# Pooling attention, then a token-mixing MLP on one core: the first batch loads and pools v in another way

## The chip, the cores and the metric

The kernel runs on one core of a Trainium2 chip. The metric is the device time of one execution in microseconds (us). The kernel before takes 377.52 us, the median of three runs (377.23 to 377.54). The core has five engines that work side by side, each through its own queue in order: TensorE (PE in the profile, PEld for its weight loads), VectorE (DVE), ScalarE (ACT), GpSimd (POOL) and SyncE (SP), which issues most transfers. ScalarE and GpSimd can issue transfers as well.

## The reference

The inputs are q, k and v of shape 8 x 8 x 576 x 64 (batch, heads, tokens, head size) and the weights of a small MLP block. Tokens of k and v are averaged in groups of eight, so each of the 576 queries attends to 72 pooled keys. Then tokens are mixed by a 576 x 576 matrix, and an MLP of 512 to 2048 to 512 follows.

```python
def _attn_ref(q, k, v):
    B, H, S, D = q.shape          # 8, 8, 576, 64
    pool = 8
    Sp = S // pool                # 72
    k_p = k.reshape(B, H, Sp, pool, D).mean(axis=3)
    v_p = v.reshape(B, H, Sp, pool, D).mean(axis=3)
    scores = 1.0 / np.sqrt(D) * np.matmul(q, k_p.transpose(0, 1, 3, 2))
    scores = scores - np.max(scores, axis=-1, keepdims=True)
    attn = np.exp(scores)
    attn = attn / (np.sum(attn, axis=-1, keepdims=True) + 1e-09)
    return np.matmul(attn, v_p).astype(np.float32)

def _moe_ref(x, alpha1, beta1, w_tok, alpha2, beta2, w_ch1, w_ch2, lam):
    a1 = alpha1 * x + beta1
    tok = np.einsum('ts,bsd->btd', w_tok, a1)
    u = x + lam * tok
    a2 = alpha2 * u + beta2
    ch = np.maximum(a2 @ w_ch1, 0.0) @ w_ch2
    return (u + lam * ch).astype(np.float32)
```

## The kernel before

Every batch passes through the same steps. Names in the profile are those of the tiles in this code. The attention steps of one batch (`u` is a half of the heads, `hp` a pair of heads, `h` a head):

```python
def load_qk(b, u, behind=None):            # q and k of four heads, tokens 0 to 511
    raw = work.tile([P, 2, 4, 4, D], FP, tag="qk_raw", bufs=2, name="qk_raw")
    if behind is not None:
        behind.memset(raw[:, :, 0, 0, 0:1], 0.0)     # keeps the load behind this point of a queue
    for i, src in enumerate((q, k)):
        nc.sync.dma_start(...)
# load_rem: tokens 512 to 575 of q and k, all heads, four small transfers on SyncE

def load_v(b, u, parts=(0, 1)):            # v in f32, one group of 8 tokens on a partition: 72 partitions
    if parts[0] == 0:
        st1[b]["v"][u] = work.tile([SPG, 4, 8, D], FP, tag="v_u", bufs=2, name="v_u")
    ...
        nc.sync.dma_start(...)

def cast_q(b, u, copy): ...                # q to bf16
def sum_k(b, u, eng):                      # four neighbouring tokens of k become one
    eng.tensor_tensor(out=raw[:, :, 0:2], in0=raw[:, :, 0:2], in1=raw[:, :, 2:4], op=ALU.add)
    eng.tensor_tensor(out=bf, in0=raw[:, :, 0], in1=raw[:, :, 1], op=ALU.add)

def att_F(b, hp): ...                      # q transposed on TensorE, copied to qT by ScalarE
def att_Frem(b, us, copy): ...             # the same for tokens 512 to 575
def att_K(b, u, copy): ...                 # k pooled and transposed by TensorE, copied to kpT

def att_V(b, hp):                          # eight tokens of v become one, by three sums on VectorE
    t = st1[b]["v"][hp // 2][:, 2 * (hp % 2):2 * (hp % 2) + 2]
    for n in (4, 2):
        nc.vector.tensor_tensor(out=t[:, :, 0:n], in0=t[:, :, 0:n], in1=t[:, :, n:2 * n], op=ALU.add)
    nc.vector.tensor_tensor(out=vp1_pool[hp][:, :, 0:64], in0=t[:, :, 0], in1=t[:, :, 1], op=ALU.add)

def att_S(b, h):                           # scores, exp on ScalarE
    ET = ET_pool[2 * r + hh]               # four score buffers
    ...
def att_AV(b, h):                          # scores times pooled v, divided by their sum on VectorE
    ...
    nc.vector.reciprocal(out=rec, in_=av[:, :, 64:65])
    nc.vector.tensor_tensor(out=x[:, :, dd:dd + D], in0=av[:, :, 0:64], in1=rec..., op=ALU.mult)
def att_X(b, h0, h1, eng=nc.vector): ...   # xs = x * lam * alpha1, in bf16, for the token mixing
```

`mix_T` mixes the tokens of one chunk on TensorE (it needs all of xs), adds x on VectorE (`u_sb`) and scales by alpha2 (`u_bf`); `mix_uT` transposes the chunk; `mlp_A` is the first product of the MLP, `mlp_B` the second, in four parts, of which part g needs `w2[g]`. `scale_w2(g)` multiplies `w2[g]` by lam on VectorE:

```python
def scale_w2(g):
    nc.vector.tensor_tensor(out=w2[g], in0=w2[g],
                            in1=lam_bc.unsqueeze(1).to_broadcast((P, 4, DM)), op=ALU.mult)
```

The first batch has a program of its own, the head of the kernel. Its transfers are issued as q, k, v (main), remainders, v (rest), q, k, v on SyncE, with alpha1, lam, beta1, alpha2 and beta2 on GpSimd's queue:

```python
broadcast(1, lamal_bc)                     # a vector to all partitions, by TensorE
cast_q(0, 0, nc.vector.tensor_copy)
att_F(0, 0); att_F(0, 1)
broadcast(0, lam_bc)
sum_k(0, 0, nc.gpsimd)
for i, p0 in ((0, 64), (1, 0)):            # the row beta1 * lam of xs
    nc.vector.tensor_tensor(out=xs_pool[i][p0:p0 + 1, 4, :], ...)
cast_rem(0, nc.gpsimd, nc.vector.tensor_copy)
att_Frem(0, (0,), nc.vector.tensor_copy)
att_K(0, 0, nc.scalar.copy)
for h in range(4):
    att_S(0, h)
nc.vector.tensor_tensor(out=lamal_bc, in0=lamal_bc, in1=lam_bc, op=ALU.mult)
load_wtok()
att_V(0, 0); att_V(0, 1)
broadcast(2, al2_bc); setup_vectors()
for h in range(4):
    att_AV(0, h)
sum_k(0, 1, nc.gpsimd)
for g in range(4): load_w1(g)              # cast to bf16 by GpSimd's transfers
for g in range(4): load_w2(g)
cast_q(0, 1, nc.scalar.copy)
att_F(0, 2); att_Frem(0, (1,), nc.scalar.copy); att_F(0, 3); att_K(0, 1, nc.scalar.copy)
att_X(0, 0, 2); att_X(0, 2, 4)
att_V(0, 2); att_V(0, 3)
# ... scores and products of heads 4 to 7, w_tok transposed, att_X(0, 4, 6, nc.gpsimd), att_X(0, 6, 8)
mix_T(0, 0, nc.gpsimd); ...; mix_T(0, 1, nc.gpsimd); mix_T(0, 2); mix_T(0, 3)
# ...
load_qk(1, 0, nc.vector); load_rem(1); load_v(1, 0); load_qk(1, 1); load_v(1, 1)
# ... mlp_A(0, 0) to mlp_A(0, 3)
```

From then on the steps of the next batch are woven into the MLP of the one before, by slots: a list of (slot, step) is sorted and run in that order. The slots of batch 1, and of w2, in the first MLP block (`n == 0`, `b == 1`):

```python
todo = [(11.9, cast_rem)]
for u in range(2):
    at = 10.0 + 4.8 * u                    # cast_q at `at`, sum_k at `at + 0.1`, on GpSimd
    for r in range(2):
        at = 12.7 + 4.6 * u + 1.6 * r      # att_F at `at`, att_V at `at + 0.5`,
                                           # for r == 1 att_Frem at + 0.1, att_K at + 0.4 (VectorE copies)
for h in range(8):
    at = 17.0 + 0.9 * h                    # att_S at `at`, att_AV 1.6 later, att_X after each odd head
                                           # (on GpSimd for h < 5, else on VectorE)
for c in range(5):
    at = 26.2 + 0.9 * c                    # mix_T
# mlp_A(0, j) at slot j from 4 on, mlp_B(0, m) part p at 16 + 4 * p + m, mix_T(0, 4) at 11.4
for g in range(4):
    todo.append((4.2 + 1.7 * g, lambda g=g: scale_w2(g)))
```

Of the kernel before, what the change touches and what calls it, by code (L numbers as in the profile page):

```python
# [14 lines left out]
P = 128  # L15
SPG = 72
# [7 lines left out]
def kernel(  # L24
# [100 lines left out]

    wt_bf = const.tile([P, 5 * S + 64], BF, tag="wt_bf", name="wt_bf")
    nc.vector.memset(wt_bf[:, 4 * S:], 0.0)
# [11 lines left out]
    vecs = const.tile([65, 4, DM], FP, tag="vecs", name="vecs")  # L139
# [4 lines left out]
    nc.gpsimd.memset(start, 0.0)  # L144
    nc.scalar.activation(out=start[:, 1:2], in_=start[:, 0:1], func=AF.Exp, bias=0.0, scale=1.0)
    new_batch(0)
    load_qk(0, 0)
    load_v(0, 0, (0,))
    load_rem(0)
    load_v(0, 0, (1,))  # L150
    load_qk(0, 1)
    load_v(0, 1)


    for i, src in ((1, moe_alpha1), (0, moe_lam)):
        n = 65 if i in (0, 3) else 1
        nc.gpsimd.dma_start(out=vecs[0:n:64, i],
                            in_=src.unsqueeze(0).to_broadcast((1 + n // 65, DM)))
# [6 lines left out]
    nc.vector.memset(pool_main, 0.125)  # L165
    pool_each = const.tile([P, 32, 4], BF, tag="pool_each", name="pool_each")
# [4 lines left out]
    for t, n, width in ((pool_main, 64, 2),):  # L171
        nc.gpsimd.affine_select(out=t, in_=t, compare_op=ALU.is_ge, fill=0.0, base=0,
                                pattern=[[-width, n]], channel_multiplier=1)
        nc.gpsimd.affine_select(out=t, in_=t, compare_op=ALU.is_ge, fill=0.0, base=width - 1,
                                pattern=[[width, n]], channel_multiplier=-1)
    each4 = pool_each.rearrange("p (g a) j -> p g a j", a=4)
# [4 lines left out]
                            fill=1.0, base=0, pattern=[[-1, P]], channel_multiplier=1)  # L181
    nc.vector.memset(ones_bf, 1.0)
# [3 lines left out]

    nc.gpsimd.dma_start(out=vecs[0:65:64, 3], in_=moe_beta1.unsqueeze(0).to_broadcast((2, DM)))
    nc.gpsimd.dma_start(out=vecs[0:1, 2], in_=moe_alpha2.unsqueeze(0))
    nc.gpsimd.dma_start(out=b2row, in_=moe_beta2.rearrange("(c p) -> c p", p=P))

    vp1_pool, kpT_pool, ET_pool = [], [], []
    for i in range(4):
        t = const.tile([SPG, 2, 66], F16, tag=f"vp1_{i}", name=f"vp1_{i}")
        nc.vector.memset(t, 8.0)
        vp1_pool.append(t)
        if i < 2:
            t = const.tile([P, 2, 2, SPG], BF, tag=f"kpT_{i}", name=f"kpT_{i}")
            nc.vector.memset(t, 0.0)
            kpT_pool.append(t)
        t = const.tile([SPG, S + 128], F16, tag=f"ET_{i}", name=f"ET_{i}")  # L200
        nc.vector.memset(t[:, 0:64], 1.0)
        nc.vector.memset(t[:, 64 + S:], 1.0)
        ET_pool.append(t)
# [10 lines left out]
    nc.vector.tensor_reduce(out=pool_rem, in_=pool_each, op=ALU.max, axis=AX.X)  # L214
# [80 lines left out]
    def att_F(b, hp):  # L295


        st = st1[b]
        u, r = hp // 2, hp % 2
        ps_q = gp("ps_q").bitcast(BF)  # L300
        for c in range(4):
            nc.tensor.transpose(  # L302
                out=ps_q[:, 128 * c:128 * c + 128],
                in_=st["q"][u][:, c, 2 * r:2 * r + 2].rearrange("p h d -> p (h d)"),
                identity=identity_bf)
        if r == 0:
            st["qT"][u] = work.tile([P, 2 * S], BF, tag="qT", bufs=4, name="qT")
        nc.scalar.copy(out=st["qT"][u][:, 640 * r:640 * r + 512], in_=ps_q[:, 0:512])
# [39 lines left out]

    def att_S(b, h):
        st = st1[b]  # L350
        u, r, hh = h // 4, h // 2 % 2, h % 2
        ET = ET_pool[2 * r + hh]
# [131 lines left out]
    new_batch(1)  # L484
    broadcast(1, lamal_bc)
    cast_q(0, 0, nc.vector.tensor_copy)
    att_F(0, 0)
    att_F(0, 1)
    broadcast(0, lam_bc)
    sum_k(0, 0, nc.gpsimd)  # L490
    for i, p0 in ((0, 64), (1, 0)):
        nc.vector.tensor_tensor(out=xs_pool[i][p0:p0 + 1, 4, :], in0=vecs[p0:p0 + 1, 3],
                                in1=vecs[p0:p0 + 1, 0], op=ALU.mult)
    cast_rem(0, nc.gpsimd, nc.vector.tensor_copy)
    att_Frem(0, (0,), nc.vector.tensor_copy)
    att_K(0, 0, nc.scalar.copy)
    for h in range(4):
        att_S(0, h)
    nc.vector.tensor_tensor(out=lamal_bc, in0=lamal_bc, in1=lam_bc, op=ALU.mult)
    load_wtok()  # L500
    att_V(0, 0)
    att_V(0, 1)
    broadcast(2, al2_bc)
    setup_vectors()
    for h in range(4):
        att_AV(0, h)
    sum_k(0, 1, nc.gpsimd)
    for g in range(4):
        load_w1(g)
    for g in range(4):  # L510
        load_w2(g)
    cast_q(0, 1, nc.scalar.copy)
    att_F(0, 2)
    att_Frem(0, (1,), nc.scalar.copy)
    att_F(0, 3)
    att_K(0, 1, nc.scalar.copy)
    att_X(0, 0, 2)
    att_X(0, 2, 4)
    att_V(0, 2)
    att_V(0, 3)  # L520
    for h in (4, 5, 6):
        att_S(0, h)
    att_AV(0, 4)
    att_S(0, 7)
    att_AV(0, 5)
    setup_wtok(0, nc.scalar.copy)
    att_X(0, 4, 6, nc.gpsimd)
    setup_wtok(1, nc.scalar.copy)
    att_AV(0, 6)
    att_AV(0, 7)  # L530
    setup_rowsum(0)
    setup_wtok(2, nc.scalar.copy)
    setup_rowsum(1)
    setup_wtok(3, nc.scalar.copy)
    att_X(0, 6, 8)
# [4 lines left out]
    mix_T(0, 2)  # L540
    mix_T(0, 3)
# [5 lines left out]
    load_rem(1)  # L547
    load_v(1, 0)
    load_qk(1, 1)
# [44 lines left out]
    for n in range(NBLK):  # L594
# [7 lines left out]
        if n == 0:  # L602
# [5 lines left out]
            for g in range(4):  # L608
                todo.append((4.2 + 1.7 * g, lambda g=g: scale_w2(g)))
# [43 lines left out]
```

The softmax here doesn't subtract the row's maximum and nothing guards it: scores larger than these inputs give would overflow.

## Time and profile before

| engine | busy us | share of the span | instructions |
|---|---|---|---|
| TensorE | 357.1 | 95% | 2283 |
| TensorE weight loads | 194.3 | 51% | 2283 |
| VectorE | 228.4 | 61% | 462 |
| ScalarE | 187.8 | 50% | 382 |
| GpSimd | 78.0 | 21% | 94 |

The profile's span is 377.4 us. The inputs read from memory are 38.04 MB, and the profile gives 126 GB/s over the span for reads and writes together. A share of busy time is an average over stages that have different limits; the chain that ended last, the waits and the busy time by stretches say what limits each stage. In a timeline line the columns are the start, the duration, the engine, the line of the kernel, the operation with its output and input tiles and shapes, how many instructions are merged, and in brackets the idle time before them with what ended it. In the chain they are start, duration, engine, tile and line.

### The profile page before, as it was taken

Reading aid. Unit: us, or ns where it says so; the run is one execution under the profiler, and the core shown is the slowest. Engines: PE = TensorE matmul, PEld = TensorE weight load, DVE = VectorE, ACT = ScalarE, POOL = GpSimd, SP = SyncE. Lnnn points to the kernel's source line nnn. Section 1 sums busy time; section 2 is a strip of 40 time slices with the busy share of each in tenths; the row PEclk is TensorE's granted clock in tenths of the full one; section 3 lists DMA queues with packets and bytes.
Section 4 is the critical chain, followed back from the end, with each engine's and each line's share of the span. In section 5 each row is a group of like instructions: output and inputs, shape, how many; then the busy total and the mean of one; then the engine's idle time right before and its main releaser. Section 6 shows DMA issues by size and latency. Waiting matters only on the chain.

```text
span 377.4 us, 5931 instructions
## 1 busy us (share of the span) xinstructions
PE 357.1 (95%) x2283; PEld 194.3 (51%) x2283; DVE 228.4 (61%) x462; ACT 187.8 (50%) x382; POOL 78.0 (21%) x94
## 2 busy tenths in 40 slices
PE   2879999799999999999999999999999999999995
PEld 0465655355655555555545554455455544544542
DVE  4797748785687569748964697469755784011011
ACT  1574766128822792269415941586148613712710
POOL 7563243900700070008000700071000000000000
PEclk9999999899999999999999999999999999999999
DMA  8999999418430753156315632383100001002012
GB/s 199 226 191 213 263 208 259 92 56 265 113 105 36 213 138 83 57 174 168 90 58 154 188 91 57 103 237 92 56 30 0 29 29 57 0 30 83 0 48 65
DMA packets 34845, 43.02 MB, mean 114 GB/s; under 512 B 2360, under 2 KB 24956, under 8 KB 34816
## 3 DMA queue, kind: packets, MB, share of 16 engines
q1 hardware_dynamic: 31744, 37.76, 36.7%
q0 software_dynamic: 3072, 4.87, 7.3%
q8 instruction: 18, 0.29, 0.4%
q14 instruction: 11, 0.09, 0.1%
HBM read 38.04 MB, written 9.44 MB: 126 GB/s over the span
## 4 chain that ended last, share of the span: by engine, by line
PE 87%; DVE 8%; DMA 2%; issue 1%; POOL 1%; ACT 0%; POOLq 0%; DVEq 0%
PE ps_h L452 33%; PE ps_ch L470 31%; PE ps_tok L421 12%; PE ps_sc L356 4%; PE ps_uT L436 2%; DMA vecs<-in_moe_beta_dram 2%; PE ps_av L372 2%; PE ps_q L302 2%; DVE x_tm L380 2%; DVE v_u L344 2%; DVE xs L387 1%; DVE vp L346 1%; DVE u_sb L423 1%; DVE u_bf L425 1%; PE ps_bias L290 1%
## 5 line engine op out<-in xcount | busy, mean ns | idle before, releaser
L470 PE MATMUL ps_ch<-w,Hj 128*128 128x512 bf16 x576 | 140.7, 380 | 0.0
L452 PE MATMUL ps_h<-u_fm,w 128*128 128x512 bf16 (+2 forms) x592 | 133.6, 373 | 0.0
L457 ACT ACTIVATE Hj<-ps_h,bias_cols 128x512 bf16<-128x512 f32 x144 | 98.8, 689 | 43.5 <-PE ps_h L452 42.6
L452 PEld LDWEIGHTS <-w 128*128 128x128 bf16 x592 | 64.0, 114 | 48.6 <-issue 0.3
L470 PEld LDWEIGHTS <-Hj 128*128 128x128 bf16 x576 | 54.5, 98 | 50.8 <-issue 1.6
L438 ACT COPY u_fm<-ps_uT 128x512 bf16<-128x512 bf16 x36 | 21.1, 586 | 94.3 <-PE ps_uT L436 94.1
L475 DVE TENSOR_TENSOR u_sb<-u_sb,ps_ch 128x512 f32<-128x512 f32 x36 | 24.5, 684 | 55.7 <-PE ps_ch L470 55.5
L358 ACT ACTIVATE ET<-ps_sc 72x288 f16<-72x288 f32 x128 | 44.9, 408 | 19.6 <-PE ps_sc L356 19.5
L421 PE MATMUL ps_tok<-xs,wtT 128*128 128x512 bf16 (+1 forms) x200 | 50.5, 385 | 2.6 <-DVE xs L387 2.6
L423 DVE TENSOR_TENSOR u_sb<-x_tm,ps_tok 128x512 f32<-128x512 f32 (+1 forms) x40 | 27.5, 687 | 30.7 <-PE ps_tok L421 30.5
L344 DVE TENSOR_TENSOR v_u<-v_u 72x512 f32<-72x512 f32 x64 | 43.2, 674 | 2.6 <-DMA v_u<-in_v_dram 1.1
L380 DVE TENSOR_TENSOR x_tm<-ps_av,rec 128x320 f32<-128x320 f32 x64 | 31.5, 492 | 2.3
L107 POOL CAST rem_q<-rem_raw 128x256 bf16<-128x256 f32 x7 | 3.7, 528 | 140.6 <-PE ps_h L452 92.5
L421 PEld LDWEIGHTS <-wtT 128*128 128x128 bf16 (+1 forms) x200 | 19.4, 99 | 25.9 <-DVE xs L387 2.5
L338 DVE CAST kpT<-ps_kp 64x144 bf16<-64x144 f32 x28 | 8.5, 305 | 38.4 <-PE ps_kp L334 38.2
L356 PE MATMUL ps_sc<-qT,kpT 128*72 128x288 bf16 x128 | 27.9, 308 | 1.6 <-ACT kpT L338 1.3
L425 DVE TENSOR_TENSOR u_bf<-u_sb,al_bc 128x512 bf16<-128x512 f32 (+1 forms) x38 | 26.6, 700 | 1.5
L372 PEld LDWEIGHTS <-ET 72*128 72x128 f16 x256 | 16.7, 102 | 14.5 <-issue 0.9
L121 POOL TENSOR_TENSOR qk_raw<-qk_raw 128x512 f32<-128x512 f32 x16 | 23.0, 1437 | 5.4 <-DMA qk_raw<-in_k_dram 5.4
L387 DVE TENSOR_TENSOR xs<-x_tm,lamal_bc 128x512 bf16<-128x512 f32 x29 | 21.4, 739 | 0.9
L114 POOL CAST q_bf<-qk_raw 128x1024 bf16<-128x1024 f32 x14 | 16.4, 1175 | 13.9 <-DMA qk_raw<-in_q_dram 13.9
L372 PE MATMUL ps_av<-vp,ET 72*128 72x66 f16 x256 | 18.6, 199 | 0.6 <-DVE vp L346 0.6
(95 smaller groups left out, 245.0 us busy)
## 6 DMA issues: line engine op xcount, KB each, us to landing
qk_raw<-in_q_dram SPq DMA_DIRECT2D x16, 512.0 KB, 5.0
qk_raw<-in_k_dram SPq DMA_DIRECT2D x16, 512.0 KB, 6.6
v_u<-in_v_dram SPq DMA_DIRECT2D x16, 512.0 KB, 7.7
out_dram<-u_sb SPq DMA_DIRECT2D x32, 256.0 KB, 2.4
w<-in_moe_w_ch_dram POOLq DMA_DIRECT2D x8, 512.0 KB, 12.8
rem_raw<-in_q_dram SPq DMA_DIRECT2D x16, 64.0 KB, 10.2
rem_raw<-in_k_dram SPq DMA_DIRECT2D x16, 64.0 KB, 4.6
v_u<-in_v_dram SPq DMA_DIRECT2D x16, 64.0 KB
```

Source lines behind the costliest of these rows:

```text
L344: nc.vector.tensor_tensor(out=t[:, :, 0:n], in0=t[:, :, 0:n], in1=t[:, :, n:2 * n], op=ALU.add)
L356: nc.tensor.matmul(out=ps_sc[0:SPG, 0:288], lhsT=kpT_pool[u][:, hh, r, :], rhs=st["qT"][u][:, S * r + n0:S * r + n0 + 288])
L358: nc.scalar.activation(out=ET[:, 64 + n0:64 + n0 + 288], in_=ps_sc[0:SPG, 0:288], func=AF.Exp, bias=0.0, scale=0.125)
L372: nc.tensor.matmul(out=av[:, c, :], lhsT=ET[:, m0:m0 + 128], rhs=vp1[:, hh, :])
L380: nc.vector.tensor_tensor(out=x[:, :, dd:dd + D], in0=av[:, :, 0:64], in1=rec.unsqueeze(2).to_broadcast((P, 5, D)), op=ALU.mult)
L387: eng.tensor_tensor(out=xs[:, 0:4, cols], in0=x[:, 0:4, cols], in1=lamal_bc[:, cols].unsqueeze(1).to_broadcast((P, 4, D * (h1 - h0))), op= ...
L421: nc.tensor.matmul(out=ps_tok, lhsT=wtT[0:kk, at, t0:t0 + P], rhs=xs[0:kk, sc, :], start=(sc == 0), stop=(sc == 4))
L423: nc.vector.tensor_tensor(out=s["u"][p0:p1, :], in0=st1[b]["x"][p0:p1, c, :], in1=ps_tok[p0:p1, 0:DM], op=ALU.add)
L425: eng.tensor_tensor(out=s["u_bf"][p0:p1, :], in0=s["u"][p0:p1, :], in1=al2_bc[p0:p1, :], op=ALU.mult)
L452: nc.tensor.matmul(out=ps_h[:, t0:t1], lhsT=w1_of(cc, j), rhs=u_fm[n][:, cc, t0:t1], start=(cc == 0), stop=(cc == 3))
L457: nc.scalar.activation(out=t, in_=ps_h, func=AF.Relu, bias=bias_cols[:, j:j + 1], scale=1.0)
L470: nc.tensor.matmul(out=ps, lhsT=Hj[n, j][:, 128 * m:128 * m + 128], rhs=w2[j // 4][:, j % 4, :], start=(j == 0), stop=(j == NJ - 1))
```

## The change

The change concerns the first batch and the loads around it.

- v of the first batch is loaded on GpSimd's queue, which casts it to f16 on the way, on 128 partitions with four neighbouring tokens each. TensorE then pools it by matmuls with two small matrices of ones (`first_V`), and VectorE copies the result out of PSUM. The three sums of `att_V` are gone for this batch.
- k of the first batch is summed by VectorE instead of GpSimd, and some copies and products change engines.
- The vectors (alpha1, lam, beta1, alpha2, beta2) are loaded from ScalarE's queue, so that GpSimd's queue is free for v, w_tok and w1.
- Each head has its own score buffer `ET`, so that scores of heads 4 to 7 needn't wait for the products of heads 0 to 3.
- w_tok and w1 are issued earlier, w2 later, its scaling later as well, and the loads of batch 1 are put in another order (v behind q and k).

It is meant to shorten the head by taking work from VectorE and by loading first what is used first. The diff, with cuts marked:

```diff
+    def load_first_v():
+        t = work.tile([P, 6, H, D], F16, tag="v_u", bufs=2, name="v_first")
+        main, rest = ...                                  # cut: two views of t
+        for u in range(2):
+            nc.gpsimd.dma_start(
+                out=main[:, 4 * u:4 * u + 4].rearrange("p h c d -> p h (c d)"),
+                in_=v[0, 4 * u:4 * u + 4, 0:512, :].rearrange("h (p c) d -> p h (c d)", c=4))
+        nc.gpsimd.dma_start(out=rest.rearrange("p h c d -> p h (c d)"),
+                            in_=v[0, :, 512:576, :].rearrange("h (p c) d -> p h (c d)", c=2))
...
-    vecs = const.tile([65, 4, DM], FP, tag="vecs", name="vecs")
+    vecs = work.tile([65, 4, DM], FP, tag="v_u", bufs=2, name="vecs")
...
+    def load_vector(i, src):
+        n = 65 if i in (0, 3) else 1
+        nc.scalar.dma_start(out=vecs[0:n:64, i],
+                            in_=src.unsqueeze(0).to_broadcast((1 + n // 65, DM)))
+    load_vector(1, moe_alpha1)
+    load_vector(0, moe_lam)
     nc.scalar.activation(out=start[:, 1:2], in_=start[:, 0:1], func=AF.Exp, bias=0.0, scale=1.0)
     new_batch(0)
     load_qk(0, 0)
-    load_v(0, 0, (0,))
     load_rem(0)
-    load_v(0, 0, (1,))
     load_qk(0, 1)
-    load_v(0, 1)
-    for i, src in ((1, moe_alpha1), (0, moe_lam)):        # and beta1, alpha2, beta2 further down
-        nc.gpsimd.dma_start(out=vecs[0:n:64, i], ...)
+    load_vector(3, moe_beta1)
+    load_vector(2, moe_alpha2)
+    nc.scalar.dma_start(out=b2row, in_=moe_beta2.rearrange("(c p) -> c p", p=P))
...                                                        # cut: pool_v, pool_vr, memsets
+    load_first_v()
...
+    load_wtok()
...
+    for i in range(H):
         t = const.tile([SPG, S + 128], F16, tag=f"ET_{i}", name=f"ET_{i}")
...
+    def first_V(u):
+        main, rest = st1[0]["v"]
+        ps_v = gp("ps_v")
+        vp = ps_v[0:SPG, 0:4 * D]
+        heads = slice(4 * u, 4 * u + 4)
+        for c in range(4):
+            nc.tensor.matmul(out=vp, lhsT=pool_v, rhs=main[:, heads, c], start=(c == 0), stop=False)
+        for c in range(2):
+            nc.tensor.matmul(out=vp, lhsT=pool_vr, rhs=rest[:, heads, c], start=False, stop=(c == 1))
+        for r in range(2):
+            nc.vector.tensor_copy(out=vp1_pool[2 * u + r][:, :, 0:64], in_=...)
...
-        ET = ET_pool[2 * r + hh]
+        ET = ET_pool[h]
...
     new_batch(1)
+    cast_q(0, 0, nc.vector.tensor_copy)
     broadcast(1, lamal_bc)
-    ...                                                   # cut: the order shown above
+    broadcast(0, lam_bc)
+    sum_k(0, 0, nc.vector)
+    att_F(0, 0); att_F(0, 1)
+    setup_pool_rem()
+    cast_rem(0, nc.vector)
+    cast_q(0, 1, nc.vector.tensor_copy)
+    att_Frem(0, (0,), nc.scalar.copy)
+    att_K(0, 0, nc.scalar.copy)
+    att_S(0, 0); att_S(0, 1)
+    sum_k(0, 1, nc.vector)
+    att_F(0, 2, nc.vector.tensor_copy)
+    att_Frem(0, (1,), nc.vector.tensor_copy)
+    att_S(0, 2)
+    att_F(0, 3, nc.vector.tensor_copy)
+    att_K(0, 1, nc.vector.tensor_copy)
+    att_S(0, 3)
+    first_V(0)
+    for g in range(4):
+        load_w1(g)
     nc.vector.tensor_tensor(out=lamal_bc, in0=lamal_bc, in1=lam_bc, op=ALU.mult)
+    att_S(0, 4); att_AV(0, 0); att_AV(0, 1); att_S(0, 5)
+    first_V(1)
+    att_AV(0, 2); att_S(0, 6); att_AV(0, 3)
+    att_X(0, 0, 2, nc.gpsimd)
+    att_S(0, 7); att_AV(0, 4)
     broadcast(2, al2_bc)
     setup_vectors()
     att_AV(0, 5)
     setup_wtok(0, nc.scalar.copy)
+    att_X(0, 2, 4, nc.gpsimd)
+    for i, p0 in ((0, 64), (1, 0)):
+        nc.gpsimd.tensor_tensor(out=xs_pool[i][p0:p0 + 1, 4, :], ...)
...                                                        # cut: AV 6 and 7, w_tok, row sums
+    att_X(0, 4, 6)
     att_X(0, 6, 8)
...
     mix_T(0, 1, nc.gpsimd)
     mix_T(0, 2)
+    for g in range(4):
+        load_w2(g)
     mix_T(0, 3)
...
     load_qk(1, 0, nc.vector)
     load_rem(1)
+    load_qk(1, 1)
     load_v(1, 0)
-    load_qk(1, 1)
     load_v(1, 1)
...
             for g in range(4):
-                todo.append((4.2 + 1.7 * g, lambda g=g: scale_w2(g)))
+                todo.append((11.2 + 3.6 * g, lambda g=g: scale_w2(g)))
```

## The prediction

> **What bounds the kernel now.** I read the busy table first, then the chain that ended last, then stretches of the timeline. TensorE is busy for 357.1 of 377.4 us, so time can only come from where it is not yet, or no longer, fed. The table by stretches shows two such places: the head, in which TensorE is busy for 18.16 of the first 29.4 us, and the end of the second batch's attention, near 70 us. The chain over the first 80 us has the head:
>
> ```profile
> 4.31 7.04 DMA vecs<-in_moe_beta_dram
> 11.45 0.69 DVE xs L492
> 12.17 0.82 DVE xs L492
> 12.99 0.21 DVE rem_q L107
> ...
> 14.57 0.61 DVE v_u L344
> 15.21 0.43 DVE v_u L344
> 15.66 1.24 DVE vp L346
> ...
> 28.28 0.96 DVE xs L387
> 29.25 0.14 issue
> 29.38 1.24 PE ps_tok L421 x5
> ```
>
> VectorE waits until 11.45 for the beta vector and then works almost without a gap until 29.24; only then can TensorE mix tokens. VectorE sets the end of the head. The second place, with the VectorE work before it, from the timeline (start, us, engine, line, operation, idle before):
>
> ```profile
> 36.14 2.28 DVE L280 TENSOR_TENSOR w<-w,lam_bc 128x2048 bf16<-128x2048 bf16 x1
> 38.34 6.69 DVE L280 TENSOR_TENSOR w<-w,lam_bc 128x2048 bf16<-128x2048 bf16 x3
> 51.63 0.68 DVE L423 TENSOR_TENSOR u_sb<-x_tm,ps_tok 64x512 f32<-64x512 f32 x1 [6.60 <-PE ps_tok L421]
> 53.03 1.13 DVE L344 TENSOR_TENSOR v_u<-v_u 72x512 f32<-72x512 f32 x2
> 70.74 1.65 DVE L387 TENSOR_TENSOR xs<-x_tm,lamal_bc 128x512 bf16<-128x512 f32 x1
> 72.45 2.31 PE L421 MATMUL ps_tok<-xs,wtT 128*128 128x512 bf16 x5 [2.04 <-DVE xs L387]
> ```
>
> The four w2 scalings fill VectorE from 36 to 45, it then rests 6.6 us, and from 51.6 it carries batch 1's attention; TensorE waits 2.04 us for its last product. The stretches around that wait (columns PE, PEld, DVE, ACT, POOL, clock, DMA share, GB/s):
>
> ```profile
> 45.00:50.00 5.00, 4.19 (x35) 2.33 (x34) 0.03 (x1) 2.96 (x7) 3.65 (x5) 1.00 1.10 197
> 68.00:72.50 4.50, 2.46 (x21) 1.14 (x20) 4.29 (x9) 0.13 (x1) 4.36 (x6) 1.00 0.51 100
> 72.50:76.00 3.50, 3.50 (x9) 1.26 (x10) 1.73 (x3) 0.00 (x0) 3.42 (x4) 0.51 0.02 5
> ```
>
> After the gap the granted clock is 0.51 for 3.5 us, which costs another 1.7 us or so. Last, the waits between 29.4 and 76 and the page's DMA row:
>
> ```profile
> POOL q_bf L114 <- DMA qk_raw<-in_q_dram: 13.9, 2, 9.5
> DVE v_u L344 <- DMA v_u<-in_v_dram: 1.1, 1, 1.1
> ```
>
> ```profile
> DMA  8999999418430753156315632383100001002012
> ```
>
> A slice is 9.4 us: the DMA engines are full from about 3 to 66 us. Batch 1's loads, issued at 36.26, queue behind w2: its last packets move at about 41, q is there at 43.8, the last v at 59.6. So early loads are a common stock, and what is loaded later must fit before its user.
>
> **What the skill says.** "DMA: Bandwidth & Descriptors", section "Issuing engines are not separate DMA queues": transfers issued by SP, ScalarE and GpSimd run on the same 16 engines and interleave. The trace agrees and is harsher: between 37 and 39 us the hardware queue moved no packet while w2 ran. Moving the vectors to ScalarE's queue thus helps by issuing first, not by more bandwidth. "VectorE: DVE Perf Modes", section "The perf-mode tier table", gives tensor_tensor on fp32 the plain rate only; the 128x512 product here takes 0.68 us. "TensorE: Matmul & The Clock Gate", section "What's actually happening", has the clock lowered after an idle window; here 0.51 followed a wait. "Trace analysis" asks for the most-contended engine of each regime (title "Perfetto Trace Analysis", section "Optimization Strategy"): here VectorE, in both places, although TensorE leads the whole.
>
> **The change part by part.**
>
> *Vectors.* In the old kernel alpha was issued at 1.37 by GpSimd and landed 5.8 us later, behind q and k. Issued by ScalarE first, I estimate 3.5 us, so the two broadcasts (2.05 us each on TensorE) end near 7.5 instead of 12.2, and beta leaves the chain.
>
> *v.* Each of the four att_V calls is a 72x512 and a 72x256 sum (0.68 and 0.42 to 0.61 us) and a cast (0.29 to 1.24), 6.9 us of VectorE by the head's rows. In their place stand four PSUM copies, about 0.25 each by the 64x144 cast of 0.30: 1.0. TensorE's twelve small matmuls cost about 2 us where it has room. The transfer writes f16 on 128 partitions instead of f32 on 72; v moved at about 205 GB/s before (1.18 MB, 5.8 us), and cast transfers also write 205 to 213 GB/s of the smaller type, so 2.9 us of DMA is saved.
>
> *Moved to VectorE:* two sum_k (0.68 + 0.42 each: 2.2), q's second cast 0.76, rem_k 0.25, two F copies 1.2, K copies 0.6, more memsets 0.7. *Moved off it:* the beta rows 1.5 and two of three wide att_X (0.96 each), against one that comes back: net 1.0.
>
> *Sum for the head.* VectorE's bound becomes second k, then the tail of work behind it. That k was summed at 15.28; with v out of its queue and no wait for a free slot I expect 13.5 (11.5 to 15), v's cast transfer taking back part. Behind it: sum 1.1, copies 0.6 + 0.3 + 0.6 + 0.6, first_V 0.5, lamal 0.7, eight AV at 0.68 = 5.4, first_V 0.5, att_X 1.9: 12.2, ending at 25.7. Tokens are mixed at about 26 instead of 29.4: 3.4 us gained. ScalarE and TensorE have under 10 us of work behind k and stay beside it; own score buffers allow that.
>
> *w2 goes late.* It used to be issued at 21 to 23. Now it stands on GpSimd's queue after the second u_bf, which ended at 34.3: 31 after the gain. Batch 1's q and k are issued at 36.3 - 3.4 = 33. W1's last byte is there at about 27 to 28 (2.1 MB at 210 GB/s: 10 us, behind q, k, v and w_tok), so the engines lie idle 4 us and do later what they did at once. W2's 2.1 MB take 10 us: 32.5 to 42.5. Batch 1 follows with v behind both q and k: 2.1 MB at about 360 GB/s (5.8), the remainder rows (2), first v at 205 (2.9), landing 1.2: 54.4, or later at the pace the old run showed. I take 56 for the first v.
>
> *Scaling goes late.* Scale 0 falls into the rest before 50, but VectorE then reaches att_V(1,0) at 53.0 - 3.4 = 49.6 and stands in order until 56. Behind it: four att_V 6.3, K copies 1.3, three scalings at 2.28 = 6.8, eight AV 5.4, two att_X 1.9: about 22. VectorE ends at 78 and TensorE cannot mix batch 1 before, against 72.45: 5.5 us later. If v came in time the same sum would end at 49.6 + 22 = 71.6, or 72.5 with the slowed att_X of 1.65 us: nothing lost, and almost nothing of the 3.4 kept.
>
> From there on TensorE is dense, with the same instructions, so a delay or gain at 72 us reaches the end. Weighing the late v at two thirds (+5.5) and the timely one at a third (0), I put the whole at +4.
>
> **The rivals.**
>
> *The head's gain lasts* (374): it needs VectorE to have slack in 50 to 72. For it: it was idle about 5 us there. Against it: 6.8 us of scaling is put in.
>
> *K and the shared engines spoil the head* (380 to 383 even without the second place): v, w_tok and w1 now enter the queue while q and k of the second half are under way, and the cast v has small packets. For it: w2 starved q completely. Against it: those loads are issued after k, and the old one already waited for v's 1.18 MB.
>
> *w2 itself is late* (over 385): scale 3 stands at slot 22 and part 3 of the second product at 28. For it: w2 shares with all of batch 1. Against it: w2 is issued first, and first served in the old run.
>
> **Range and chances.** The centre is 377.5 + 4 = 381.5. With v in time and k early it can be 375.5; with v at 59 and a low clock in the longer gap, 387. Over 2% faster needs 370: more than the head gains in my sum. Over 2% slower needs 385.1: first v two to four us later than I think. So 0.05, 0.82, 0.13.
>
> **What would show it.** First token mix at 25 to 28; no beta wait at VectorE; GB/s near zero between 28 and 32; a VectorE wait of 4 to 8 us for v near 50; scalings in between the attention products at 56 to 73; batch 1's first token mix at 75 to 80 behind a VectorE product and a low clock behind that; equal stages from 90 on but for the shift. I am wrong if v for batch 1 lands before 50, or VectorE's ops between 50 and 75 sum to under 20 us, or the first mix comes before 24.

## The result and the profile after

The changed kernel takes 394.12 us, the median of four runs (393.76 to 394.61). The kernel before took 377.53 us beside it (377.23 to 378.81). The ratio is 1.043, with an interval of 1.041 to 1.045: slower by 16.6 us, where 4 us were predicted and at most 9.5 us allowed for.

TensorE's busy time and the DMA row of the page after, in slices of 9.8 us:

```profile
PE 362.2 (92%) x2295; PEld 196.4 (50%) x2295; DVE 224.8 (57%) x473; ACT 186.0 (47%) x377; POOL 79.2 (20%) x91
...
DMA  9980499920743174307420842094100011002011
```

VectorE's work falls only from 228.4 to 224.8 us, TensorE's rises by 5.1 us. The DMA row has a hole in its fourth slice, where the kernel before was full. The chain that ended last after, over its first 100 us (start, us, engine, tile and line), shows where the time went:

```profile
1.38 4.53 DMA vecs<-in_moe_lam_dram
5.92 0.54 SPq L87
...
7.29 15.00 DMA qk_raw<-in_k_dram
22.31 0.70 DVE qk_raw L121
...
31.02 2.00 PE ps_bc L245 x2
...
37.34 2.09 PE ps_tok L463 x5
...
58.20 8.62 DMA v_u<-in_v_dram
67.01 0.70 DVE v_u L370
...
69.06 2.29 DVE w L306
...
74.11 2.20 DVE w L306
```

The second half's k is on the way from 7.29 to 22.31 (the first two lines are taken up at the end). The beta vector, which held VectorE before, is gone from the chain, as intended. Tokens are first mixed at 37.34 instead of 29.38: **8.0 us lost in the head.** Later v of batch 1 comes at 67.01, and scalings of w2 stand among the attention work behind it. From the timeline after (start, us, engine, line, operation, idle before), with three issues of the head:

```profile
5.05 0.61 POOL L143 DMA_DIRECT2D wt_bf<-in_moe_w_tok_dram  x1
...
6.50 0.75 SPq L77 DMA_DIRECT2D qk_raw<-in_q_dram  x1
7.29 0.57 SPq L77 DMA_DIRECT2D qk_raw<-in_k_dram  x1
...
67.01 1.14 DVE L370 TENSOR_TENSOR v_u<-v_u 72x512 f32<-72x512 f32 x2 [4.69 <-DMA v_u<-in_v_dram]
...
88.43 1.02 PE L463 MATMUL ps_tok<-xs,wtT 128*128 128x512 bf16 x4 [3.10 <-DVE xs L429]
```

Batch 1's tokens are mixed at 88.43 instead of 72.45, 16.0 us later. Taking off the 8.0 of the head leaves **8.0 us lost in the second place.** Behind it nothing more is lost: 304.5 of the span of 392.9 us remain, against 304.9 of 377.4 before, in the two profiled executions. The waits of the first 110 us after (engine, line, what it waited for; total, times, longest):

```profile
DVE rem_k L108 <- DMA rem_raw<-in_k_dram: 5.2, 1, 5.2
...
DVE v_u L370 <- DMA v_u<-in_v_dram: 4.7, 1, 4.7
...
DVE q_bf L114 <- DMA qk_raw<-in_q_dram: 3.9, 1, 3.9
```

With the 3.5 us ahead of the second k, VectorE now stands 12.5 us in the head for loads. Stretches after (columns PE, PEld, DVE, ACT, POOL, clock, DMA share, GB/s):

```profile
26.00:29.40 3.40, 3.40 (x26) 2.17 (x26) 2.59 (x9) 1.41 (x4) 1.03 (x1) 1.00 0.16 26
29.40:36.00 6.60, 6.60 (x53) 4.92 (x52) 4.33 (x14) 3.83 (x9) 4.84 (x6) 1.00 0.01 2
36.00:45.00 9.00, 8.84 (x73) 5.22 (x72) 5.44 (x11) 3.37 (x10) 4.40 (x6) 1.00 0.09 7
```

The DMA engines move 2 to 26 GB/s for nearly 19 us: w1 had ended early, and w2 was issued only at 43.09, behind a head that was late.

Two theories stood after this. **A:** the weights (w_tok and w1, cast on GpSimd's queue) run beside q, k and the remainders of the second half and take their share, so k is late; this is the rival that the prediction named and set aside. **B:** the head is late by its new order of work, and k's lateness is hidden anyway. For the second place, three causes were to be told apart: w2 arriving late, its scaling standing late, and the shift by the head alone.

### The profile page after: what moved, and what is told of

It is laid out like the page before. It is cut to its first block, busy times and chain, and to the rows that moved or that the text cites. A ratio compares the mean times of both kernels' runs of the same rounds, so it can differ in the third digit from the quotient of the medians.

```text
span 392.9 us, 6027 instructions
## 1 busy us (share of the span) xinstructions
PE 362.2 (92%) x2295; PEld 196.4 (50%) x2295; DVE 224.8 (57%) x473; ACT 186.0 (47%) x377; POOL 79.2 (20%) x91
## 4 chain that ended last, share of the span: by engine, by line
PE 83%; DMA 7%; DVE 7%; issue 0%; SPq 0%; ACT 0%; ACTq 0%; DVEq 0%
PE ps_h L494 31%; PE ps_ch L512 29%; PE ps_tok L463 11%; PE ps_sc L398 4%; DMA qk_raw<-in_k_dram 4%; DMA v_u<-in_v_dram 2%; PE ps_av L414 2%; PE ps_uT L478 2%; DVE w L306 2%; PE ps_q L328 1%; DMA vecs<-in_moe_lam_dram 1%; DVE x_tm L422 1%; DVE v_u L370 1%; DVE xs L429 1%; DVE u_sb L465 1%; DVE u_bf L467 1%
## 5 line engine op out<-in xcount | busy, mean ns | idle before, releaser
L370 DVE TENSOR_TENSOR v_u<-v_u 72x512 f32<-72x512 f32 (+1 forms) x56 | 38.7, 690 | 6.1 <-DMA v_u<-in_v_dram 4.7
L398 PE MATMUL ps_sc<-qT,kpT 128*72 128x288 bf16 x128 | 29.3, 310 | 4.8 <-DVE kpT L364 3.3
L107 POOL CAST rem_q<-rem_raw 128x256 bf16<-128x256 f32 x7 | 4.7, 667 | 136.5 <-DMA rem_raw<-in_q_dram 136.5
L121 POOL TENSOR_TENSOR qk_raw<-qk_raw 128x512 f32<-128x512 f32 x14 | 20.6, 1474 | 0.8 <-DMA qk_raw<-in_k_dram 0.8
L429 DVE TENSOR_TENSOR xs<-x_tm,lamal_bc 128x512 bf16<-128x512 f32 x28 | 19.7, 704 | 0.9
L114 POOL CAST q_bf<-qk_raw 128x1024 bf16<-128x1024 f32 x14 | 15.3, 1096 | 12.9 <-DMA qk_raw<-in_q_dram 12.9
## 6 DMA issues: line engine op xcount, KB each, us to landing
w<-in_moe_w_ch_dram POOLq DMA_DIRECT2D x8, 512.0 KB, 12.6
```

What stands on the lines that cost most here:

```text
L398: nc.tensor.matmul(out=ps_sc[0:SPG, 0:288], lhsT=kpT_pool[u][:, hh, r, :], rhs=st["qT"][u][:, S * r + n0:S * r + n0 + 288])
```

## The experiments

All experiments compute the whole reference. Each is compared with the kernel before on the same chip. That kernel's median lay between 377.5 and 378.6 in the four groups of runs, so a difference between experiments of different groups is good to about 1 us.

**Weights behind k.** A copy of one element by GpSimd reads the second k, and so holds w_tok and w1 until k has landed. Against the changed kernel:

```diff
-    load_wtok()                              # at the start
...
     first_V(0)
+    nc.gpsimd.tensor_copy(out=start[:, 0:1], in_=st1[0]["raw"][1][0:1, 1, 3, 3, 0:1])
+    load_wtok()
     for g in range(4):
         load_w1(g)
```

> Changed kernel, but the transfers of w_tok and w1 are issued only once the second k of batch 0 has landed. Theory (these weights, on the same 16 engines, hold back the second q and k): the second k is summed at 13 to 16 us instead of 22.3, the first token mix comes at 28 to 31 instead of 37.3, and the whole falls by 6 to 9 us to 385 to 388; the 8 us lost in batch 1 stay. Rival (the late issue of the second q and k at 6.5 and 7.3, or v's own cast transfer, holds them back): the second k stays at 20 or later and the time within 2 us of 394.

Measured: 385.68 us (384.94 to 386.09), ratio 1.020 (1.015 to 1.024). Its timeline:

```profile
13.86 0.69 DVE L121 TENSOR_TENSOR qk_raw<-qk_raw 128x512 f32<-128x512 f32 x1 [0.65 <-DMA qk_raw<-in_k_dram]
...
22.51 2.07 PE L244 MATMUL ps_bc<-vecs,ones_row 1*128 1x512 f32 x2
...
28.89 1.24 PE L462 MATMUL ps_tok<-xs,wtT 128*128 128x512 bf16 x5 [0.17 <-DVE xs L428]
...
58.04 1.14 DVE L369 TENSOR_TENSOR v_u<-v_u 72x512 f32<-72x512 f32 x2 [5.43 <-DMA v_u<-in_v_dram]
...
79.45 1.02 PE L462 MATMUL ps_tok<-xs,wtT 128*128 128x512 bf16 x4 [1.76 <-DVE xs L428]
```

The second k is summed at 13.86 instead of 22.31, and tokens are mixed 8.45 us earlier. The time falls by 8.4 us. Theory A holds, and B falls: the same order of work, with k in time, reaches the mixing at 28.89. The second place is untouched: batch 1 still mixes 50.6 us behind the first mixing (43.1 before).

**W1 alone behind k.** The same copy, but w_tok stays at the start:

```diff
     first_V(0)
+    nc.gpsimd.tensor_copy(out=start[:, 0:1], in_=st1[0]["raw"][1][0:1, 1, 3, 3, 0:1])
     for g in range(4):
         load_w1(g)
```

> Changed kernel, with only w1 held until the second k of batch 0 has landed; w_tok goes early as in the change. Theory (w1's packets take turns with those of the second q and k, one for one, from 12 us on): the second k is summed at 15.5 to 17.5, the time is 387 to 389, so w1 makes about 6 and w_tok about 2 of the 8.4 us that holding both gave. Rival (w_tok, larger packets, does most of it): the second k later than 19 and 391 or more.

Measured: 389.35 us (387.39 to 391.04), ratio 1.028 (1.023 to 1.034). Its timeline:

```profile
17.15 0.69 DVE L121 TENSOR_TENSOR qk_raw<-qk_raw 128x512 f32<-128x512 f32 x1 [0.65 <-DMA qk_raw<-in_k_dram]
...
31.00 1.24 PE L463 MATMUL ps_tok<-xs,wtT 128*128 128x512 bf16 x4 [1.32 <-DVE xs L429]
```

Of the 8.45 us by which k was late, 22.31 - 17.15 = 5.2 are w1's and 17.15 - 13.86 = 3.3 are w_tok's, taken away in this order. The time lies a little above what was expected, and about halfway between the changed kernel and the one with both held.

**w2 early, scaled early.** w2 is issued right behind w1 and scaled at the old slots:

```diff
         load_w1(g)
+    for g in range(4):
+        load_w2(g)
...
     mix_T(0, 2)
-    for g in range(4):
-        load_w2(g)
...
-                todo.append((11.2 + 3.6 * g, lambda g=g: scale_w2(g)))
+                todo.append((4.2 + 1.7 * g, lambda g=g: scale_w2(g)))
```

> Changed kernel, but w2 is issued directly behind w1 and scaled at the slots of the kernel before. Theory (the late w2 and its late scaling cost about 8 us in batch 1, apart from the head): first token mix unchanged at about 37, batch 1's first token mix at about 80 instead of 88.4, time 384 to 388. Rival (everything after the head only inherits the head's delay, or the wait is for batch 1's v whatever w2 does): 391 to 394.

Measured: 384.68 us (384.52 to 386.55), ratio 1.019 (1.014 to 1.023). Its timeline:

```profile
36.05 1.24 PE L463 MATMUL ps_tok<-xs,wtT 128*128 128x512 bf16 x5 [1.32 <-DVE xs L429]
...
59.68 1.13 DVE L370 TENSOR_TENSOR v_u<-v_u 72x512 f32<-72x512 f32 x2
...
78.82 1.25 PE L463 MATMUL ps_tok<-xs,wtT 128*128 128x512 bf16 x5 [2.03 <-DVE xs L429]
```

The head is late as before, but the way from the first mixing to batch 1's is 42.8 us, as in the old kernel, and no bracket stands at v: it had come. So the second place lost its time through w2's two moves, not through the head's shift.

**The same two moves in the kernel before.** The reverse of that edit, in the old kernel:

```diff
         load_w1(g)
-    for g in range(4):
-        load_w2(g)
...
     mix_T(0, 2)
+    for g in range(4):
+        load_w2(g)
...
-                todo.append((4.2 + 1.7 * g, lambda g=g: scale_w2(g)))
+                todo.append((11.2 + 3.6 * g, lambda g=g: scale_w2(g)))
```

> Kernel before, with only w2 issued late and scaled late as the change does; head and load order as before. Theory: head unchanged at 29.4, batch 1's first token mix 6 to 9 us later than 72.45, time 383 to 387. Rival (late w2 only hurts behind the changed head): 377 to 379.

Measured: 387.12 us (385.01 to 387.79), ratio 1.023 (1.018 to 1.028). Its timeline:

```profile
56.71 1.14 DVE L344 TENSOR_TENSOR v_u<-v_u 72x512 f32<-72x512 f32 x2 [2.62 <-DMA v_u<-in_v_dram]
...
80.21 1.79 PE L421 MATMUL ps_tok<-xs,wtT 128*128 128x512 bf16 x5 [3.22 <-DVE xs L387]
```

With the old head (first mixing at 29.54) the two moves cost 8.5 us. The loss of the second place is shown in both kernels. Batch 1's loads stand here in their old order, half of v ahead of the second q and k, and its mixing still comes 50.7 us behind the first, so their new order isn't the cause.

**The two moves apart.** First the scaling early alone, with w2 late, in the changed kernel:

```diff
-                todo.append((11.2 + 3.6 * g, lambda g=g: scale_w2(g)))
+                todo.append((4.2 + 1.7 * g, lambda g=g: scale_w2(g)))
```

> Changed kernel, w2 still issued late, but scaled at the old slots, so that VectorE does all four before batch 1's attention. Theory (VectorE's sum behind the wait for v sets batch 1's end): v still lands near 67, the 6.8 us of three scalings are gone from behind it, first token mix of batch 1 at 82 to 84 instead of 88.4, time 387 to 390. Rival (the late v alone sets it): 392 or more. Rival (the scalings, waiting for the late w2, stand in front of batch 1's work): later than 394.

Measured: 388.74 us (387.91 to 391.16), ratio 1.028 (1.023 to 1.033). VectorE scales as w2 lands, at 46.42, 50.37, 53.10 and 55.98, in time in which it had waited; v comes at 65.06 and batch 1 mixes at 81.57:

```profile
65.06 1.24 DVE L370 TENSOR_TENSOR v_u<-v_u 72x512 f32<-72x512 f32 x2 [4.12 <-DMA v_u<-in_v_dram]
...
81.57 1.41 PE L463 MATMUL ps_tok<-xs,wtT 128*128 128x512 bf16 x5 [2.04 <-DVE xs L429]
```

Then w2 early alone, with the scaling late:

```diff
         load_w1(g)
+    for g in range(4):
+        load_w2(g)
...
     mix_T(0, 2)
-    for g in range(4):
-        load_w2(g)
```

> Changed kernel, w2 issued behind w1 but scaled at the late slots. Theory (with v in time, VectorE still has some 22 us of work from about 59.7 on): batch 1's first token mix at 81 to 83 against 78.8 with the scaling early too, time 386.5 to 389. Rival (late scaling costs nothing once v is in time): 384 to 385.5.

Measured: 390.96 us (390.94 to 393.07), ratio 1.035 (1.030 to 1.040), 2 us above what was expected. Its timeline:

```profile
61.08 1.13 DVE L370 TENSOR_TENSOR v_u<-v_u 72x512 f32<-72x512 f32 x2
...
83.43 1.84 PE L463 MATMUL ps_tok<-xs,wtT 128*128 128x512 bf16 x5 [3.10 <-DVE xs L429]
```

v had come when VectorE reached it at 61.08, and yet batch 1 mixes only at 83.43, after 22.35 us of VectorE work with the scalings in it. With the scaling early the same way takes 19.1 us (59.68 to 78.82 above). Of the 6.3 us between these two kernels 3.2 lie here, 1.4 in the head (first mixing at 37.45), most of it because TensorE ran slower there in this execution (last section), and the rest behind the mixing, at a low clock that is told of below.

So from 394.1 the early scaling alone brings 5.4 us, the early w2 alone 3.2, both together 9.4. These times also hold what TensorE's pace did in the head and behind the mixing. The way from the first mixing to batch 1's leaves that out: it is 51.1 us in the changed kernel, 45.3 with the scaling early, 46.0 with w2 early and 42.8 with both. So the two moves are worth 5.8 and 5.1 us alone and 8.3 together: each takes one of two obstacles away, v's lateness or the scalings behind v, and they overlap in part.

**Both places mended.** The edits of the first and the third experiment together, so w_tok, w1 and w2 behind k and the scaling early:

```diff
-    load_wtok()                              # at the start
...
     first_V(0)
+    nc.gpsimd.tensor_copy(out=start[:, 0:1], in_=st1[0]["raw"][1][0:1, 1, 3, 3, 0:1])
+    load_wtok()
     for g in range(4):
         load_w1(g)
+    for g in range(4):
+        load_w2(g)                           # and no longer behind mix_T(0, 2)
...
-                todo.append((11.2 + 3.6 * g, lambda g=g: scale_w2(g)))
+                todo.append((4.2 + 1.7 * g, lambda g=g: scale_w2(g)))
```

> Changed kernel with both: w_tok, w1 and w2 issued once the second k has landed, and the scaling at the old slots. Theory (two separate losses of 8 us each): they add, 376 to 380. If the head keeps a real gain from the lighter VectorE, 373 to 376. Rival (the losses overlap, one cause): 384 or more.

Measured: 378.25 us (376.63 to 379.90, 20 runs), ratio 1.000 (0.999 to 1.002). The losses are undone, 15.9 us of them, yet what remains of the change is no gain that can be measured. Its timeline shows a head that is in time and then stumbles:

```profile
13.89 0.69 DVE L121 TENSOR_TENSOR qk_raw<-qk_raw 128x512 f32<-128x512 f32 x1 [0.64 <-DMA qk_raw<-in_k_dram]
...
20.64 1.12 PE L244 MATMUL ps_bc<-vecs,ones_row 1*128 1x512 f32 x2
...
25.40 3.13 POOL L571 TENSOR_TENSOR xs<-vecs 1x512 bf16<-1x512 f32 x2
26.00 1.34 DVE L432 TENSOR_TENSOR xs<-x_tm,lamal_bc 64x128 bf16<-64x128 f32 x1
26.22 1.02 PE L462 MATMUL ps_tok<-xs,wtT 128*128 128x512 bf16 x4 [1.81 <-DVE xs L428]
27.49 0.59 PE L462 MATMUL ps_tok<-xs,wtT 65*128 65x512 bf16 x1 [0.24 <-DVE xs L432]
```

The first mixing starts at 26.22, as predicted for the change. The 64x128 product of its last piece takes 1.34 us, where its like took 0.28 in the first kernel with the weights held; GpSimd makes the two beta rows at that time (the line at 25.40). Then the granted clock falls to 0.64 for 4 us. The MLP starts at 35.52 against 36.73 before, and batch 1 mixes at 70.94 against 72.45.

**Idle matmuls and another place for the beta rows.** On top of the last kernel, the two beta rows on VectorE in its wait for the second q, `keep_warm(6)` (matmuls whose result nobody reads) ahead of the first mixing and `keep_warm(8)` ahead of batch 1's:

```diff
     setup_pool_rem()
+    for i, p0 in ((0, 64), (1, 0)):
+        nc.vector.tensor_tensor(out=xs_pool[i][p0:p0 + 1, 4, :], ...)   # was on nc.gpsimd, further down
     cast_rem(0, nc.vector)
...
+    keep_warm(6)
     mix_T(0, 0, nc.gpsimd)
...
+            todo.append((26.1, lambda: keep_warm(8)))
```

> The version with w_tok, w1 and w2 behind the second k and early scaling, and in it the two beta rows on VectorE in its wait for the second q instead of on GpSimd at the end of the head, six idle matmuls ahead of the first token mix and eight ahead of batch 1's, to keep the clock up. Theory (the 3 us gained in the head are lost to slowed VectorE products beside GpSimd's and to the low clock after the waits): 373 to 375.5. Rival (the clock records are no real loss, or the gain goes elsewhere): 376 to 378.5.

Measured: 378.08 us (375.05 to 379.88, 20 runs), ratio 0.997 (0.995 to 0.999): in the rival's range. The executions fall into two groups, nine from 375.05 to 377.14 and eleven from 378.05 to 379.88; what parts them is not shown, and the profile is of one of the nine. Batch 1's mixing keeps clock 1.00, but the first mixing moved to 28.49. The chain behind k there is TensorE's from 15.98 to 25.24 but for one step of ScalarE, at a clock of 0.60 from 24 to 28 us, and four of the idle matmuls stand in it. So a part of TensorE's work was taken out of that chain:

```diff
     att_Frem(0, (0,), nc.scalar.copy)
+    broadcast(2, al2_bc)                     # alpha2 to all partitions: before k is there
+    setup_vectors()
...
     att_AV(0, 4)
-    broadcast(2, al2_bc)
-    setup_vectors()
...
-    keep_warm(6)
+    keep_warm(2)
     mix_T(0, 0, nc.gpsimd)
```

> The version with the weights behind the second k, early scaling, beta rows on VectorE and eight idle matmuls ahead of batch 1's mix, with the alpha2 broadcast and the beta2 transpose moved out of the end of the head into TensorE's wait for the remainder rows, and two idle matmuls instead of six ahead of the first mix. Theory (TensorE at the low clock was the bound of that head behind 16 us): first token mix at 25 to 27 instead of 28.5, time 373 to 375.5, ratio to the kernel before 0.990 to 0.996. Rival (VectorE or the loads of batch 1 take over): no better than 0.997.

Measured: 375.68 us (374.55 to 376.59, 14 runs), ratio 0.994 (0.992 to 0.996). This is the best version, and it beats both kernels, by 2.1 us the one before. Time and first mixing (27.46 against 25 to 27) come a little later than expected. Its timeline:

```profile
13.78 0.69 DVE L121 TENSOR_TENSOR qk_raw<-qk_raw 128x512 f32<-128x512 f32 x1 [0.64 <-DMA qk_raw<-in_k_dram]
...
27.46 1.63 PE L462 MATMUL ps_tok<-xs,wtT 128*128 128x512 bf16 x5
...
70.74 1.24 PE L462 MATMUL ps_tok<-xs,wtT 128*128 128x512 bf16 x5 [0.41 <-DVE xs L428]
```

The first mixing comes 1.0 us earlier than with six idle matmuls and the broadcast in the chain, and 1.9 us earlier than in the kernel before. But the lower group of the version before it has a median of 375.33, so a gain in time from moving the broadcast itself is not shown.

**Second q and k ahead of the remainders.** On top of that one, the second q and k are issued before the remainder rows, and VectorE takes them in that order:

```diff
     load_qk(0, 0)
-    load_rem(0)
     load_qk(0, 1)
+    load_rem(0)
...
-    cast_rem(0, nc.vector)
     cast_q(0, 1, nc.vector.tensor_copy)
+    sum_k(0, 1, nc.vector)
+    att_F(0, 2, nc.vector.tensor_copy)
+    att_F(0, 3, nc.vector.tensor_copy)
+    cast_rem(0, nc.vector)
```

> The same with the second q and k issued ahead of the remainder rows, and VectorE's order to suit. Theory (rank in the queue decides when a load lands): the second k lands at 9.5 to 11.5 instead of 14, the remainder rows at 12 to 14 and become the bound; first token mix within 1 us of the version with the remainders first, time within 1 us of it. Rival (the second q and k were the only bound): first token mix 2 us or more earlier, 371 to 373.

Measured: 378.32 us (377.49 to 379.42), ratio 1.001 (0.999 to 1.003), 2.6 us more than without this edit, where at most 1 us was expected. Its timeline:

```profile
12.20 0.69 DVE L121 TENSOR_TENSOR qk_raw<-qk_raw 128x512 f32<-128x512 f32 x1 [2.32 <-DMA qk_raw<-in_k_dram]
...
13.94 0.28 DVE L107 CAST rem_q<-rem_raw 128x256 bf16<-128x256 f32 x1
...
29.29 1.26 PE L462 MATMUL ps_tok<-xs,wtT 128*128 128x512 bf16 x5 [0.98 <-DVE xs L428]
```

The second k is summed at 12.20, 1.6 us earlier, but the remainder of q is now cast at 13.94 and the one of k summed at 14.18. No bracket stands at them: they had landed, and it is VectorE's new order that puts them behind the second k. TensorE waits 3.3 us for the first, and the broadcast of alpha2, which stands behind it on TensorE, moves from ahead of k to 14.67. The first mixing is at 29.29, 1.8 us later. One wait was exchanged for another.

**Idle matmuls in the kernel before.** The old kernel with the idle matmuls of batch 1 and nothing else:

```diff
+            todo.append((26.1, lambda: keep_warm(8)))
```

> Kernel before, with only eight idle matmuls put ahead of batch 1's first token mix, in TensorE's wait for VectorE. Theory (the wait of 2.04 us is followed by 3.5 us at half clock, worth 1.7): the clock from 72.5 to 76 stays at 0.9 or more, time 1 to 2 us lower, ratio 0.995 to 0.998. Rival (the slow stretch is one that the clock takes anyway): ratio 0.999 to 1.002.

Measured: 377.39 us (376.78 to 378.87), ratio 0.999 (0.997 to 1.000). No gain is shown. The clock behind batch 1's mixing is 1.00 instead of 0.51 in its profile, but in that execution v came late and the mixing began at 73.99, so the two profiles don't tell what the clock alone is worth. The other executions do, in part. In this group the kernel before has a mean granted clock of 0.994 or 0.995 in 7 of 35 executions, which take 378.95 us in the median, and 0.998 or more in the other 28, which take 377.64. Its profile, at 0.994, is of the first kind. With the idle matmuls none of 14 lies below 0.997. So the low clock goes with some 1.3 us, but in a fifth of the executions only, and the median has little to gain. That it is the stretch behind the mixing in each of them is inferred from the one profile.

## Why the prediction was wrong, point by point

**The step that failed is "second k, 13.5 (11.5 to 15)"** in the head's sum. It was summed at 22.31. The packets of GpSimd's queue (q0) and of SyncE's (q1) in the changed kernel, for 14 to 16 us; below the dots q0 for 22 to 24 us, when k is there; and last both for 50 to 52 us, when w2 runs beside batch 1's loads (packets, MB, share of 16 engines):

```profile
q0 software_dynamic: 240, 0.25, 72.0%
q1 hardware_dynamic: 240, 0.25, 44.2%
...
q0 software_dynamic: 414, 0.41, 123.9%
...
q0 software_dynamic: 94, 0.32, 82.1%
q1 hardware_dynamic: 98, 0.10, 18.0%
```

From 12 to 20 us the two queues take turns, one packet each, and GpSimd's, which cast on the way, take 72.0 / 44.2 = 1.6 times as long. The load that VectorE waits for gets 0.25 MB in 2 us, about 125 GB/s, while weights needed much later get as much. The Trainium skill says so: "DMA: Bandwidth & Descriptors", section "Queues, rings and completion order", has each DMA engine go round the queues at packet granularity, and the trace agrees for these 8 us. It doesn't before: from 6 to 10 us, while v's cast transfer ran, q0 moved 1226 packets and q1 257, though the remainder of k and the second q had been issued; what holds q1 back there stays open. The prediction cited the same page for sharing the engines, but didn't draw from it how much a load loses.

The rival "K and the shared engines spoil the head" was this cause, with its size (380 to 383) too small: with only the second place mended the time is 384.68. The argument against it was "those loads are issued after k". It is wrong twice: w_tok was issued at 5.05 and w1's first part at 6.38, ahead of the second q at 6.50 and k at 7.29; and an earlier issue on another queue gives no precedence. It also drew on the old head, where the second half waited for v's transfer, but on its own queue.

**"12.2 us of work behind k" was 15.0** (22.31 to 37.34, and 13.86 to 28.89 with the weights held). VectorE's items have their predicted sizes, 0.68 a product and 0.49 + 0.18 for each head. What failed is that TensorE, said to have "under 10 us of work behind k", would "stay beside it": between 23.5 and 37.0 us it is busy for 13.45 of 13.5, and the chain is TensorE's up to 35.05. The twelve matmuls that pool v, which were to cost 2 us "where it has room", take 2.84 us of this chain, and the two broadcast matmuls for alpha2 take 2.00. TensorE also ran at half pace there (last section): with both places mended, where its pace is full from about 17 us up to the mixing, the way from k to the mixing is 12.33 us. The head's sum was therefore short by 22.31 - 13.5 = 8.8 us in k and 2.8 in the tail, less 0.3 by which the mixing had been rounded up: 11.3 us, from 26 to 37.34.

**Vectors and beta: right.** The first broadcast starts at 2.26 instead of 7.21, and no beta wait is left. It gained nothing, as k came last.

**v by TensorE: not disproved.** The four sums and casts are gone from VectorE, and its copies take 0.48 us for two. What v's own transfer costs k was not tried apart.

**w2 late: the mechanism was right, and it started late.** The DMA engines were to be idle from 28 to 32; they were for nearly all of 26 to 43, because w2 hung on the second `u_bf`, and so on the head. Everything there is later by the 11.3 us: v of batch 1 was to come at 56 and came at 67.01. With the head mended alone it came at 58.04, 2 us later than predicted. "First served" was true only for the first 4 us or so: batch 1's q was issued at 45.07, its queue moved no packet before 48 and one before 49, and from then on it took turns with w2, whose packets are larger (last two lines above: 0.32 MB against 0.10). Why the queue stood still at first, as in the old kernel, stays open.

**Scaling late: right in mechanism and size.** The sum from v to the mixing was "about 22" and measured 67.01 to 88.43, 21.4; with v in time it was to take almost all of the head's 3.4, and the two moves apart gave 3.2 (46.0 against 42.8). The wait for v was to be 4 to 8 us and was 4.69. Relative to the head this place was to lose 8.9 us (a gain of 3.4 turned into a loss of 5.5) and lost 8.0. The chance of one third that v would be in time was too kind: v was late in every run that issued w2 late.

**The low clock behind the mixing** was predicted and did not come: 1.00 after a wait of 3.10 us. In the kernel before it was no fixed cost either: the profile that was read is of one of the executions that have it.

Put together: the miss against 381.5 is 12.6 us. The k that came late explains 8.4, by the run that holds the weights; at 385.7 that run lies inside the predicted range. Of the other 4.2 us, 1.5 are the weighing of +5.5 down to +4, and 1.5 are batch 1's mixing at 79.45 in that run against 78, where v came 2 us late behind the head's longer tail. The last 1.2 fit the low clock in the profile that was read, which the forecast's base of 377.5 doesn't hold; that is not shown. The part that was meant to gain is small even when nothing spoils it: 2.1 us, with the idle matmuls.

## What to carry to other kernels

A bulk load that has time must wait for the last load that the critical chain needs, by a dependency: an earlier issue on another queue doesn't protect it, and each packet of the bulk load takes its turn. Before work is moved behind a transfer, look at who else is late there: w2's scaling cost nothing where VectorE would have waited. Three scalings behind v, 6.8 us of work, made the way from v to the mixing 4.9 us longer where v was late (21.4 against 16.5) and 3.2 where it was in time. And when an engine is relieved, add up the next one by the durations that the stage itself shows.

## What the runs showed of the hardware

**TensorE runs at half pace in much of the head, and the clock column doesn't show it at first.** The same two broadcasts take 2.07 us in the kernel with w_tok and w1 held (at 22.51) and 1.12 us in the one with w2 early as well (at 20.64), with 1.00 in the clock column both times. Seven kernels have the same work of TensorE and VectorE, in the same order, between k and the mixing. It takes 15.0 us in the three whose broadcasts take 2.07 us (the changed kernel, w_tok and w1 held, w2 early with late scaling), 13.9 in the three where they take 1.12 and the pace falls once more before the mixing (w1 held, w2 early, w2 late with early scaling), and 12.3 with both places mended, at full pace up to the mixing. That second fall does show in the column: 0.50 from 31.2 to 34.4 us with w2 early. The Trainium skill, "TensorE: Matmul & The Clock Gate", section "What's actually happening", has a half clock as the default until a window of sustained work, at a free-running phase; the factor of 1.85 agrees. That this is the cause of the 2.7 us was read from these traces and not tried by an edit.

**A wait doesn't say whether the clock falls behind it.** Two kernels wait the same 3.10 us ahead of batch 1's mixing, with TensorE busy for 0.90 of the 4 us before it. The 4 us from the mixing on, with w1 held:

```profile
82.22:86.22 4.00, 3.83 (x17) 1.57 (x18) 3.16 (x4) 0.00 (x0) 3.92 (x4) 1.00 0.01 4
```

and with w2 early and scaled late:

```profile
83.43:87.43 4.00, 4.00 (x11) 1.38 (x12) 2.51 (x3) 0.00 (x0) 3.92 (x4) 0.57 0.02 4
```

At 0.57, eleven matmuls were done instead of seventeen. Nor is it the same in every execution of one kernel, as the mean clocks of the kernel before show. In all four kernels with eight idle matmuls ahead, batch 1's mixing ran at its full pace, 1.24 us a chunk.

**An issue of SyncE waited for a load that ScalarE had issued.** In the first lines of the chain after, SyncE's issue of the remainder of k (line 87) is released at 5.92 by the landing of the lam vector, by the profile's reading; why it should wait for that isn't shown. SyncE's second q is issued at 6.50 for it, against 5.82 before, although two transfers of v less stand ahead of it on that queue.

**VectorE's product slows beside GpSimd's.** 0.28 us became 1.34 in the kernel with both places mended, beside one-partition rows on GpSimd; with those rows elsewhere it took 0.28 again.
